# Attention output held in SBUF, and three 64-column products with v in place of a 64- and a 128-column one

## The chip, the cores and the metric

The kernel runs on one core of a Trainium2 chip. The metric is the device time of one execution in microseconds (us). Five engines work side by side, each on its own in-order stream of instructions: TensorE (PE, with its weight loads listed apart as PEld), VectorE (DVE), ScalarE (ACT), GpSimd (POOL) and SyncE (SP), which here issues every DMA.

## The reference

Attention with a memory term, followed by a two-layer network whose non-linearity is a squared relu. Four batches, eight heads, 576 positions, head width 64; 2304 tokens of width 512; hidden width 2048.

```python
scores = scale * np.matmul(q, k.transpose(0, 1, 3, 2))      # causal mask, then softmax -> a
local = np.matmul(a, v)
q_p = phi(q)                                                # elu + 1
mem_out = einsum(q_p, M_prev) / (einsum(q_p, z_prev) + 1e-6)
attn = g * mem_out + (1 - g) * local                        # g = sigmoid(beta)
x = attn.transpose(0, 2, 1, 3).reshape(B * S, H * D)
out = np.maximum(x @ w_in, 0.0) ** 2 @ w_out
```

Everything is float32. The kernel reaches that precision on 16-bit operands by splitting a number into a high and a low half and adding three products (high by high, low by high, high by low).

## The kernel before, in words

**Weights.** w_in and w_out come in 32 pieces of 512 KB. A piece is loaded by SP into a `raw` buffer (L269), its 64-bit words are put together to float32 by POOL or DVE (L192, L194), ACT (L195) and DVE (L198, into an `fc` buffer), and, once four pieces have a common scale (`weight_scale`), split into fp16 halves by ACT (L241) and DVE (L242). The `raw` and `fc` buffers come from two rings: the first eight pieces use a ring of 4 `raw` and 6 `fc` buffers; later pieces mostly use a second ring (`raw2`, `fc2`) in a pool that lies where the pool `tp` of the first tokens lay, so that its buffers wait for the end of `first_tokens`.

**First tokens.** The first 64 positions of every batch are computed apart (`first_tokens`, L319 to L391) and are block 0 of the network.

**Attention.** `attention(b, p, tiles, ...)` runs for a batch, a pair of heads and two or four query tiles of 128 rows; there are 24 such calls in `order`: batches 0 and 1 in two halves of two tiles, batches 2 and 3 whole. A call makes the memory term (`memx`, L520), then for each tile the scores (L543), mask and minimum (L564, DVE), exponential (L584, ACT), two fp16 halves `a` (L622 ACT, L624 DVE), a transposing DMA to `aT` (L628), the products with v (PE), and on DVE the division by the row sum and the addition to `memx` (L664). Six of the 64 tiles, those of the first three calls, take a float32 way (`full`); the other 58 are of the kind that the change touches. For those v has the halves `vh` and `vl` side by side in `vs`: per 64 or 128 keys the low half of `a` is multiplied with `vh` (64 columns, L651) and the high half with `vh` and `vl` together (128 columns, L649 and L654); `reduce_sum` (L656) adds the two 64-column parts into `s3`, from which L664 reads.

**Hand-over.** Each pair of finished tiles is written to a DRAM tensor `xd` (L675). `token_halves` reads a block of 256 tokens back (L699, L701), takes its scale (ACT L703, DVE L212 to L707), splits it (ACT L710, DVE L711) and transposes it by DMA into `xT` (L712). `moe(n)` calls it for block n + 1 at its step `PJ` = 6 of 8, and the block before the last two does it for both of those.

**Network.** `moe(n)`: first layer (L830 to L832, three products per k), relu, square, halves (L836 to L842), second layer (L802 to L804). Blocks 1 to 6 are done one by one, the last two together in `moe_pair` (L744 to L766).

**What sets the order.** The program text sets priorities: what is written earlier goes first when both can run. `ORD` interleaves the first attention calls with weight pieces (`wsteps`) and with `moe(0)`; then all other attention is written, then `moe(1)` on. A scheduler at build time turns that into one fixed order for each engine, in which network work fills what attention leaves free. At run time each engine keeps its order, and SP too: a DMA that has to wait holds up every DMA behind it.

Of the kernel before, what the change touches and what calls it, by code (L numbers as in the profile page):

```python
# [8 lines left out]
F32 = mybir.dt.float32  # L9
F32R = mybir.dt.float32r  # L10
# [40 lines left out]
NRAW = 4  # L51
NRAW2 = 2
NFC = 6
NFC2 = 6
NR0 = 8
# [4 lines left out]
EB = 3  # L60
RB = 2
KB = 2
XB = 4
PJ = 6
# [18 lines left out]
WE2 = 6  # L83
# [11 lines left out]
VB = 2  # L95
# [3 lines left out]
def fused_kernel(ctx: ExitStack, tc: tile.TileContext, t0_d, kk_d, qv_d, beta, w_in, w_out, out):  # L99
# [75 lines left out]
    xw = {}  # L175
# [10 lines left out]
    def to_float(n):  # L186
# [9 lines left out]
        pool, tag, bufs = (rwp, "fc", NFC) if first_ring(n, NFC, NFC2) else (more[0], "fc2", NFC2)  # L196
        fc[n] = pool.tile([P, 512], F32, tag=tag, name=tag, bufs=bufs)
# [40 lines left out]
    def halves(n, sc):  # L238
        f1 = fc.pop(n)
        hi, lo = wt[n][:, 0], wt[n][:, 1]  # L240
        nc.scalar.activation(hi, f1, AF.Copy, scale=sc)  # L241
        nc.vector.scalar_tensor_tensor(out=lo, in0=f1, scalar=sc, in1=hi, op0=ALU.mult, op1=ALU.subtract)  # L242
# [12 lines left out]
    wpl = ctx.enter_context(tc.tile_pool(name="wpl", bufs=1))  # L255
    rwp = ctx.enter_context(tc.tile_pool(name="rwp", bufs=1))
    more = []

    def first_ring(n, a, b):
        return n < NR0 or (n - NR0) % (a + b) >= b  # L260

    def load_weight(n):
        wt[n] = wpl.tile([P, 2, 512], F16, name=f"w{n}")
        if first_ring(n, NRAW, NRAW2):
            raw[n] = rwp.tile([P, 1024], U32, tag="raw", name="raw", bufs=NRAW)
        else:
            raw[n] = more[0].tile([P, 1024], U32, tag="raw2", name="raw2", bufs=NRAW2)
        w, r0, cs = wsrc[n]
        nc.sync.dma_start(raw[n], w[r0 : r0 + P, cs])  # L269
# [8 lines left out]
    def weights():  # L278
        with tc.tile_pool(name="tp", bufs=1, reuse_waits="tile") as tp:
            first_tokens(tp, ahead)  # L280
        more.append(ctx.enter_context(tc.tile_pool(name="rw2", bufs=1, reuse_waits="tile")))
        yield
        for n in range(NU):
            while len(loaded) < min(NU, n + NRAW + NRAW2):
                ahead()
# [10 lines left out]

    def first_tokens(tp, ahead):
        xT = mo.tile([P, 2, 2 * NK, P], F16, tag="xT", name="xT", bufs=2)
        xq.append((xT, tok0))
# [102 lines left out]
    dp = ctx.enter_context(tc.tile_pool(name="dp", bufs=1, space=bass.MemoryType.DRAM))  # L402
    xd = [dp.tile([S, DM], F32, name=f"xd{b}") for b in range(B)]
# [14 lines left out]
    def attention(b, p, tiles, ld, after, early, sfull, full):  # L418
# [13 lines left out]
        if not sfull:  # L432
            qh, ql = (at.tile([P, SQ], F32R, tag=t, name=t) for t in ("qh", "ql"))
            kh, kl = (at.tile([P, S], F32R, tag=t, name=t) for t in ("kh", "kl"))
# [14 lines left out]
        pe = at.tile([P, 2, S], F32, tag="e", name="pe", bufs=EB)[:, 0]  # L449
# [3 lines left out]
        if lead:  # L453
            later("s2", ex)
# [14 lines left out]
        if not full:  # L469
# [15 lines left out]
            vs = at.tile([P, 2, 5, 2 * D], F16, tag="vs", name="vs", bufs=1)  # L485
# [14 lines left out]
        memx = at.tile([P, 4, P], F32, tag="memx", name="memx", bufs=VB)  # L500
# [28 lines left out]
        done, started, a12 = set(), set(), None  # L529
        row = {}  # L530

        def scores(group):
# [20 lines left out]
            for (i, ka, kb), cs in zip(group, at_col):  # L553
                q0 = QT[i][0]
                if ka == 0:
                    row[i] = (
                        at.tile([P, 2, S], F32, tag="e", name="e", bufs=EB),
# [17 lines left out]
        for i in [t for t in TORD if t in tiles]:  # L575
# [31 lines left out]
            else:  # L607
# [4 lines left out]
                else:  # L612
                    a = at.tile([P, tg * P], F16, tag=f"a{tg}", name="a")
                    aT = at.tile([P, tg, P], F16, tag=f"aT{tg}", name="aT")
# [21 lines left out]
            acc = ps.tile([P, 2, 2, D], F32, tag="av", name="acc", bufs=2)  # L636
            if full:
                s3 = acc[:, :, 0]
                for h in range(2):
                    hd = slice(h * D, (h + 1) * D)  # L640
                    for c in range(nb):
                        kp = D if c == 0 else P
                        nc.tensor.matmul(
                            acc[:n, h, 0], aT[:kp, h * nb + c, :n], v[:kp, c, hd], start=c == 0, stop=c == i
                        )
            else:
                for h in range(2):
                    o2 = acc[:n, h].rearrange("p j d -> p (j d)")
                    nc.tensor.matmul(o2, aT[:, h * nb, :n], vs[:, h, 0], start=True, stop=i == 0)  # L649
                    for c in range(1, i + 1):  # L650
                        nc.tensor.matmul(  # L651
                            acc[:n, h, 0], aT[:, h * nb + i + c, :n], vs[:, h, c, :D], start=False, stop=False
                        )
                        nc.tensor.matmul(o2, aT[:, h * nb + c, :n], vs[:, h, c], start=False, stop=c == i)  # L654
                s3 = at.tile([P, 2, D], F32, tag="s3", name="s3", bufs=1)
                nc.vector.reduce_sum(out=s3[:n], in_=acc[:n].rearrange("p h j d -> p h d j"), axis=AX.X)  # L656
            if FX[late] == "p" and not full:
                xo = memx[:n, i - 1].rearrange("p (h d) -> p h d", h=2)
                smb = sm[:n, :, None].to_broadcast([n, 2, D])
                nc.gpsimd.tensor_tensor(out=s3[:n], in0=s3[:n], in1=smb, op=ALU.mult)  # L660
                nc.gpsimd.tensor_tensor(out=xo, in0=s3[:n], in1=xo, op=ALU.add)
            for h in range(2 if FX[late] != "p" or full else 0):
                xo = memx[:n, i - 1, h * D : (h + 1) * D]
                nc.vector.scalar_tensor_tensor(  # L664
                    out=xo, in0=s3[:n, h], scalar=sm[:n, h : h + 1], in1=xo,
                    op0=ALU.mult, op1=ALU.add,
                )
            fs = slice(p * P, (p + 1) * P)
            done.add(i)
            i0 = (i - 1) // 2 * 2 + 1  # L670
            if i0 in done and i0 + 1 in done and (b, p, i0) == (0, NP - 1, 1):
                last.append(memx)
            elif i0 in done and i0 + 1 in done:
                r0 = QT[i0][0]
# [14 lines left out]
    def token_halves(b, blk, xts, out_scale, tail=None):  # L689


        nk = NK if tail is None else NK - 1
# [3 lines left out]
        for t in range(2):  # L696
            r0 = QT[1 + 2 * blk + t][0]
            src = mo.tile([P, DM], F32, tag="x", name="xn", bufs=XB)
            nc.sync.dma_start(src[:, : nk * P], xd[b][r0 : r0 + P, : nk * P])  # L699
            if tail is not None:  # L700
                nc.sync.dma_start(src[:, nk * P :], tail[:, t])  # L701
# [16 lines left out]
    def prefetch(b, blk, tail=None):  # L718
        xT = mo.tile([P, 2, 2 * NK, P], F16, tag="xT", name="xT", bufs=2)
        osc = mo.tile([P, 2], F32, tag="osc", name="osc", bufs=2)  # L720
# [261 lines left out]
```

## Time and profile before

| what | value |
|---|---|
| runs | 598.8, 599.82, 603.67 us (median 599.82) |
| profiled execution | 604.48 us, of which the span of the trace is 602.7 us |
| PE busy | 543.7 us (90%) |
| DVE busy | 427.7 us (71%) |
| ACT busy | 376.8 us (63%) |
| POOL busy | 61.8 us (10%) |

A share of busy time is a mean over stages. The first stage (to about 150 us) prepares the weights, the middle one (to about 490 us) mixes attention and network, the last one is network alone. A busy PE includes the latency of its products, which overlap; the start-to-start distance of products tells what they cost.

### The profile page before, as it was taken

Reading aid. Unit: us, or ns where it says so; the run is one execution under the profiler, and the core shown is the slowest. Engines: PE = TensorE matmul, PEld = TensorE weight load, DVE = VectorE, ACT = ScalarE, POOL = GpSimd, SP = SyncE. Lnnn points to the kernel's source line nnn. Section 1 sums busy time; section 2 is a strip of 40 time slices with the busy share of each in tenths; the row PEclk is TensorE's granted clock in tenths of the full one; section 3 lists DMA queues with packets and bytes.
Section 4 is the critical chain, followed back from the end, with each engine's and each line's share of the span. In section 5 each row is a group of like instructions: output and inputs, shape, how many; then the busy total and the mean of one; then the engine's idle time right before and its main releaser. Section 6 shows DMA issues by size and latency. Waiting matters only on the chain.

```text
span 602.7 us, 11893 instructions
## 1 busy us (share of the span) xinstructions
PE 543.7 (90%) x4341; PEld 365.1 (61%) x4341; DVE 427.7 (71%) x1407; ACT 376.8 (63%) x831; POOL 61.8 (10%) x41
## 2 busy tenths in 40 slices
PE   6566988978989899998989999988999998999997
PEld 6455765645767666666666676656775775444443
DVE  6947888899986889799779696787977733222221
ACT  2535978559776868788688587588785634322223
POOL 2723872100010100000000000000000000000000
PEclk9975997889989999999999999999999999999999
DMA  8716962574966777796774764858826451000001
GB/s 315 258 63 202 369 203 75 141 146 93 187 136 142 131 161 148 151 173 129 203 149 114 123 149 103 163 129 184 158 54 112 109 131 36 35 1 1 0 2 71
DMA packets 141468, 79.08 MB, mean 131 GB/s; under 512 B 114016, under 2 KB 127584, under 8 KB 141408
## 3 DMA queue, kind: packets, MB, share of 16 engines
q1 hardware_dynamic: 141408, 78.31, 55.1%
q8 instruction: 34, 0.56, 0.4%
q14 instruction: 26, 0.21, 0.1%
HBM read 41.59 MB, written 8.78 MB: 84 GB/s over the span
## 4 chain that ended last, share of the span: by engine, by line
PE 31%; DVE 25%; DMA 21%; ACT 15%; issue 5%; SPq 1%; POOL 0%; DVEq 0%; ACTq 0%; POOLq 0%
PE oacc L744 7%; DMA aT<-a 4%; DMA vv<-in_qv_dram 4%; DVE e L564 4%; DMA xn<-xd 3%; ACT e L584 3%; DVE a L624 3%; DMA xd<-memx 2%; PE up L758 2%; PE up L757 2%; PE up L759 2%; ACT a L622 2%; DMA raw<-in_w_out_dram 2%; PE up L830 2%; PE oacc L802 2%
## 5 line engine op out<-in xcount | busy, mean ns | idle before, releaser
L830 PE MATMUL up<-xT,w 128*128 128x256 f16 x448 | 123.6, 276 | 0.9 <-DMA xT<-hl 0.8
L831 PE MATMUL up<-xT,w 128*128 128x256 f16 x448 | 123.6, 276 | 0.0
L832 PE MATMUL up<-xT,w 128*128 128x256 f16 x448 | 123.1, 276 | 0.0
L584 ACT ACTIVATE e<-e,mx 128x320 f32<-128x320 f32 (+3 forms) x128 | 77.5, 606 | 53.4 <-DVE memx L664 31.1
L802 PE MATMUL oacc<-w,gh 128*128 128x512 f16 x224 | 85.5, 384 | 9.5 <-ACT gh L839 5.5
L803 PE MATMUL oacc<-w,gh 128*128 128x512 f16 x224 | 86.1, 384 | 0.5 <-DVE w L242 0.5
L804 PE MATMUL oacc<-w,gl 128*128 128x512 f16 x224 | 83.0, 386 | 2.1 <-DVE gl L842 1.7
L624 DVE SCALAR_TENSOR_TENSOR a<-e,a 128x128 f16<-128x128 f32 x116 | 64.6, 566 | 25.9 <-ACT a L622 25.2
L622 ACT ACTIVATE a<-e 128x128 f16<-128x128 f32 x116 | 55.0, 522 | 11.2 <-DMA aT<-a 10.8
L830 PEld LDWEIGHTS <-w 128*128 128x128 f16 x448 | 44.3, 99 | 13.4 <-issue 2.3
L765 DVE CAST gh<-r 128x512 f16<-128x512 f32 x16 | 6.8, 428 | 62.0 <-ACT r L764 62.0
L831 PEld LDWEIGHTS <-w 128*128 128x128 f16 x448 | 44.4, 99 | 9.9 <-issue 0.3
L832 PEld LDWEIGHTS <-w 128*128 128x128 f16 x448 | 44.3, 99 | 8.7 <-issue 1.7
L192 POOL TENSOR_SCALAR raw<-raw 128x512 uint32<-128x512 uint16 x21 | 46.2, 2199 | 32.5 <-DMA raw<-in_w_in_dram 13.2
L564 DVE CUSTOM_DVE_ANT_0 e<-sp,mask 128x320 f32<-128x320 f32 (+3 forms) x128 | 47.4, 418 | 0.1
L842 DVE TENSOR_TENSOR gl<-r,gh 128x512 f16<-128x512 f32 x56 | 39.3, 702 | 10.9 <-ACT gh L839 10.4
L763 ACT ACTIVATE r<-up,gam 128x512 f32<-128x512 f32 x16 | 11.0, 687 | 57.2 <-PE up L759 57.2
L836 ACT ACTIVATE r<-up,gam 128x512 f32<-128x512 f32 x48 | 32.3, 672 | 17.5 <-PE up L832 17.5
L802 PEld LDWEIGHTS <-gh 128*128 128x128 f16 x224 | 22.1, 99 | 28.4 <-ACT gh L839 7.2
L804 PEld LDWEIGHTS <-gl 128*128 128x128 f16 x224 | 21.9, 99 | 27.5 <-DVE gl L842 5.2
L654 PE MATMUL acc<-vs,aT 128*128 128x128 f16 x302 | 37.3, 224 | 0.0
L651 PE MATMUL acc<-vs,aT 128*128 128x64 f16 x302 | 35.9, 196 | 0.0
(175 smaller groups left out, 1174.1 us busy)
## 6 DMA issues: line engine op xcount, KB each, us to landing
raw<-in_w_in_dram SPq DMA_DIRECT2D x16, 512.0 KB, 6.3
raw<-in_w_out_dram SPq DMA_DIRECT2D x16, 512.0 KB, 5.3
vv<-in_qv_dram SPq DMA_DIRECT2D x16, 320.0 KB, 3.0
kd<-in_kk_dram SPq DMA_DIRECT2D x16, 288.0 KB, 3.1
out_dram<-o SPq DMA_DIRECT2D x16, 256.0 KB, 2.8
xd<-memx SPq DMA_DIRECT2D x31, 128.0 KB, 2.3
xn<-xd SPq DMA_DIRECT2D x14, 256.0 KB, 3.0
qm<-in_qv_dram SPq DMA_DIRECT2D x8, 321.0 KB, 3.5
```

Source lines behind the costliest of these rows:

```text
L192: nc.gpsimd.tensor_scalar(out=u0, in0=top, scalar1=2.0**-13, scalar2=7.0, op0=ALU.mult, op1=ALU.min)
L564: nc.vector.tensor_tensor_reduce(out=e[:, h, ka:kb], in0=sps[:, h, cs], in1=mask[:, 448 - q0 + ka : 448 - q0 + kb], scale=-0.125, scalar=3 ...
L584: ex = nc.scalar.activation(e[:n, h, :ke], e[:n, h, :ke], AF.Exp, bias=bs, scale=-1.0, accum_out=sm[:n, h : h + 1])
L622: nc.scalar.mul(av[:, :, o0 : o0 + w], x, SC)
L624: nc.vector.scalar_tensor_tensor(out=av[:, :, o0 + w : o0 + 2 * w], in0=x, scalar=SC, in1=av[:, :, o0 : o0 + w], op0=ALU.mult, op1=ALU.sub ...
L744: mms.append(nc.tensor.matmul(acc[t], g[:, ts], w_out_op(f, part), start=s0, stop=s1))
L802: nc.tensor.matmul(acc[t], gh[:, u, ts], w_out_op(f, 0), start=f == f0, stop=False)
L803: nc.tensor.matmul(acc[t], gh[:, u, ts], w_out_op(f, 1), start=False, stop=False)
L804: nc.tensor.matmul(acc[t], gl[:, u, ts], w_out_op(f, 0), start=False, stop=f == f1)
L830: nc.tensor.matmul(up[:, u, :], w_in_op(f, k, 0), xT[:, :, k], start=k == 0, stop=False)
L831: nc.tensor.matmul(up[:, u, :], w_in_op(f, k, 0), xT[:, :, NK + k], start=False, stop=False)
L832: nc.tensor.matmul(up[:, u, :], w_in_op(f, k, 1), xT[:, :, k], start=False, stop=k == NK - 1)
```

## The change: what it does, and the diff

Three things are changed together.

1. `acc` is one group of 64 columns per head. All three products with v, for each stretch of keys, are 64 columns wide and add into the same columns; the high half of `a` is loaded as weights twice. `reduce_sum` is gone, and L664 reads `acc` from PSUM.
2. The attention output stays in SBUF: `memx` is a slice of a tile `feat[b]` that holds a batch, and `token_halves` reads it there. The DMAs of L675, L699 and L701 are gone. `prefetch` is called where the last head pair of a block is finished, in the text of attention, and no longer in `moe`.
3. To make room, the weight buffers are in pools that close: pieces 0 to 15 use a ring of 8 `raw` and 12 `fc` buffers that is open beside `tp`, pieces 16 to 31 a ring of 6 and 8 opened after it. What is free after that is the pool `late`, from which every second attention call after the fifth takes its work tiles (`e`, `a`, `aT`, `vs` and the halves of q and k). `ORD` takes 17 and 34 pieces where it took 13 and 33.

```diff
-NRAW = 4
-NRAW2 = 2
-NFC = 6
-NFC2 = 6
-NR0 = 8
+NRAW = 8
+NRAW2 = 6
+NFC = 12
+NFC2 = 8
+NR0 = 16
...
-WE2 = 6
+WE2 = 40
...
-    merge((attn(0, 1), 12), (wsteps(13), 12))
-    merge((attn(1, FIRST), 52), (wsteps(33), 20), (first(), 18))
+    merge((attn(0, 1), 12), (wsteps(17), 16))
+    merge((attn(1, FIRST), 52), (wsteps(34), 16), (first(), 18))
...
+    def weights():
+        with tc.tile_pool(name="rw", bufs=1) as rw:
+            more.append(rw)
+            with tc.tile_pool(name="tp", bufs=1, reuse_waits="tile") as tp:
+                first_tokens(tp, ahead)
+            yield
+            yield from pieces(0, NR0, NRAW)
+        wpl.append(ctx.enter_context(tc.tile_pool(name="wpl2", bufs=1, reuse_waits="tile")))
+        with tc.tile_pool(name="rw2", bufs=1, reuse_waits="tile") as rw:
+            more.append(rw)
+            yield from pieces(NR0, NU, NRAW2)
+        more.append(ctx.enter_context(tc.tile_pool(name="late", bufs=1, reuse_waits="tile")))
+        yield
...
-        memx = at.tile([P, 4, P], F32, tag="memx", name="memx", bufs=VB)
+        if b not in feat:
+            feat[b] = mo.tile([P, 4, DM], F32, tag="feat", name="feat", bufs=HB)
+        memx = feat[b][:, :, p * P : (p + 1) * P]
...
-                    o2 = acc[:n, h].rearrange("p j d -> p (j d)")
-                    nc.tensor.matmul(o2, aT[:, h * nb, :n], vs[:, h, 0], start=True, stop=i == 0)
...
-                s3 = at.tile([P, 2, D], F32, tag="s3", name="s3", bufs=1)
-                nc.vector.reduce_sum(out=s3[:n], in_=acc[:n].rearrange("p h j d -> p h d j"), axis=AX.X)
...
+            acc = ps.tile([P, 2, D], F32, tag="av", name="acc", bufs=2)
+            for h in range(2):
+                hd = slice(h * D, (h + 1) * D)
...
+                    mms = [(aT[:, h * nb], vh[:, 0]), (aT[:, h * nb], vl[:, 0])]
+                    for c in range(1, i + 1):
+                        hi, low = aT[:, h * nb + c], aT[:, h * nb + i + c]
+                        mms += [(low, vh[:, c]), (hi, vh[:, c]), (hi, vl[:, c])]
+                for x, (lhs, rhs) in enumerate(mms):
+                    nc.tensor.matmul(acc[:n, h], lhs[:, :n], rhs, start=x == 0, stop=x == len(mms) - 1)
...
-                xw[b, p, i0] = nc.sync.dma_start(
-                    xd[b][r0 : r0 + 2 * P, fs].rearrange("(i p) f -> p i f", p=P), memx[:, i0 - 1 : i0 + 1]
                 )
...
-            src = mo.tile([P, DM], F32, tag="x", name="xn", bufs=XB)
-            nc.sync.dma_start(src[:, : nk * P], xd[b][r0 : r0 + P, : nk * P])
+            src = feat[b][:, 2 * blk + t]
...
-            elif j == PJ and n + 1 < NBLK:
-                assert n > 0 or last
-                xq.append(prefetch(*blocks[n + 1], *last))
...
-            yield from attention(*order[i], ld, after, i < NEARLY, i < NES, i < NEF and max(order[i][2]) < 4)
+            yield from attention(*order[i], ld, after, i < NEARLY, i < NES, i < NEF and max(order[i][2]) < 4, more[-1] if i > FIRST and i % 2 else at)
+            b, p, tiles = order[i]
+            if p == NP - 1:
+                need(NU + 2)
+                for blk in range(2):
+                    if 2 * blk + 1 in tiles:
+                        prefetch(b, blk)
+                yield
```

The order of the DMAs on SP changes in the weight stage. Before (`raw` with a number is the second ring; `kd`, `qm`, `vv` are inputs of an attention call; in brackets the engines or DMA queues that the DMA waits for):

```order
L269 DMA raw<-in_w_in_dram 128x1024 [waits DMAHW7_49,DMAHW3_49,DVE_49]
L269 DMA raw<-in_w_in_dram 128x1024 [waits DMAHW0_49,DMAHW4_49,DVE_49,Activation_49]
L269 DMA raw<-in_w_out_dram 128x1024 [waits DMAHW1_49,DMAHW5_49,DVE_49,Activation_49]
L269 DMA raw<-in_w_out_dram 128x1024 [waits DMAHW6_49,DMAHW2_49,DVE_49]
L408 DMA kd<-in_kk_dram 128x320 [waits PE_49]
L269 DMA raw_507<-in_w_in_dram 128x1024
L269 DMA raw_568<-in_w_in_dram 128x1024
L408 DMA kd<-in_kk_dram 128x320 [waits PE_49]
L412 DMA qm<-in_qv_dram 128x386 [waits DVE_49,DMAHW3_49,PE_49,Activation_49]
L269 DMA raw_644<-in_w_out_dram 128x1024 [waits DMAHW4_49,DMAHW0_49,DVE_49]
```

With the change (line numbers of the changed kernel: L266 is the load of a piece, L415 to L422 the inputs of attention):

```order
L266 DMA raw<-in_w_in_dram 128x1024 [waits DMAHW0_49,DVE_49]
L415 DMA kd<-in_kk_dram 128x320 [waits DMAHW1_49]
L419 DMA qm<-in_qv_dram 128x386 [waits DMAHW2_49]
L422 DMA vv<-in_qv_dram 128x384 [waits DMAHW3_49]
L266 DMA raw<-in_w_in_dram 128x1024 [waits DMAHW4_49,DVE_49]
L266 DMA raw<-in_w_in_dram 128x1024 [waits DMAHW5_49,DVE_49]
L266 DMA raw<-in_w_in_dram 128x1024 [waits DMAHW6_49,DVE_49]
L266 DMA raw<-in_w_out_dram 128x1024 [waits DMAHW7_49,DVE_49]
L266 DMA raw<-in_w_out_dram 128x1024 [waits DMAHW0_49,DVE_49]
L266 DMA raw<-in_w_out_dram 128x1024 [waits DMAHW1_49,DVE_49]
L266 DMA raw<-in_w_out_dram 128x1024 [waits DMAHW2_49,DVE_49]
L415 DMA kd<-in_kk_dram 128x320 [waits PE_49]
```

Before, twelve pieces are issued ahead of the first `kd` that waits for PE; with the change sixteen are.

On DVE the same stage, around the first attention call. Before, six conversions of pieces (L198) stand behind that call's mask steps and its memory term (L514 to L520):

```order
L194 TENSOR_SCALAR raw_568<-raw_568 128x512
L514 SCALAR_TENSOR_TENSOR nm<-pm,gi 128x4
L518 RECIPROCAL nm<-nm 128x4
L520 TENSOR_TENSOR memx<-pm,nm 128x256
L198 SCALAR_TENSOR_TENSOR fc_641<-raw_507 128x512
L198 SCALAR_TENSOR_TENSOR fc_648<-raw_568 128x512
L198 SCALAR_TENSOR_TENSOR fc_655<-raw 128x512
L198 SCALAR_TENSOR_TENSOR fc_662<-raw 128x512
L198 SCALAR_TENSOR_TENSOR fc_704<-raw 128x512
L198 SCALAR_TENSOR_TENSOR fc_798<-raw 128x512
```

With the change (L196 is the conversion, L241 the low half of a weight, L573 the mask step, L392 and L395 steps of the first tokens) eight conversions, pieces 8 to 15, stand ahead of the call's first mask step:

```order
L392 TENSOR_TENSOR xs<-xp,sn 128x512
L241 SCALAR_TENSOR_TENSOR w_619<-fc,wout_s,w_619 128x512
L241 SCALAR_TENSOR_TENSOR w_622<-fc,wout_s,w_622 128x512
L196 SCALAR_TENSOR_TENSOR fc<-raw 128x512
L471 SCALAR_TENSOR_TENSOR pe<-qm,pe 128x256
L196 SCALAR_TENSOR_TENSOR fc<-raw 128x512 x7
L395 TENSOR_TENSOR xT<-xs,xT 128x512
L225 TENSOR_REDUCE win_e<-gr 128x1
L573 ISA e,mx<-sp,mask 128x320
```

## Rows read from the trace of the kernel before

**Rows 1.** The page, part 1: busy us (share of the span) and count.

```profile
PE 543.7 (90%) x4341; PEld 365.1 (61%) x4341; DVE 427.7 (71%) x1407; ACT 376.8 (63%) x831; POOL 61.8 (10%) x41
```

**Rows 2.** Busy time of each engine by stretch, with granted clock, DMA share, GB/s.

```profile
core 0: us, PE busy (x) PEld busy (x) DVE busy (x) ACT busy (x) POOL busy (x), PEclk, DMA share, GB/s
0.00:60.00 60.00, 37.67 (x479) 31.83 (x480) 41.82 (x110) 25.30 (x52) 23.92 (x20) 0.82 0.60 209
60.00:160.00 100.00, 88.28 (x669) 63.34 (x669) 90.58 (x285) 76.26 (x175) 32.84 (x18) 0.91 0.64 172
160.00:500.00 340.00, 319.15 (x2718) 223.00 (x2716) 271.98 (x972) 245.60 (x560) 5.01 (x4) 0.99 0.67 139
500.00:603.00 103.00, 98.65 (x480) 46.89 (x480) 23.28 (x42) 29.66 (x46) 0.00 (x0) 0.99 0.07 21
```

**Rows 3.** Timeline of DVE, 27 to 56 us: start, us, instruction [idle before <-releaser].

```profile
29.71 0.68 DVE L198 SCALAR_TENSOR_TENSOR fc<-raw 128x512 uint32<-128x512 uint32 x1
...
45.06 0.29 DVE L212 TENSOR_SCALAR qn<-nm 128x128 uint32<-128x128 uint32 x1 [5.68 <-PE nm L380]
...
53.89 2.69 DVE L198 SCALAR_TENSOR_TENSOR fc<-raw 128x512 uint32<-128x512 uint32 x4
```

**Rows 4.** Waits of the SP queue in the first 60 us: total, times, longest.

```profile
SPq L408 <- PE nm L380: 14.3, 1, 14.3
```

**Rows 5.** Waits of PE between 160 and 500 us.

```profile
PE oacc L802 <- ACT gh L839: 3.5, 5, 1.6
...
PE pm L509 <- DVE s L656: 1.5, 3, 0.6
PE vt L478 <- DVE s L656: 1.0, 2, 0.8
...
PE up L830 <- DMA xT<-hl: 0.8, 1, 0.8
```

**Rows 6.** Groups by line and shape: busy us, mean ns of one, idle before.

```profile
L656 DVE TENSOR_REDUCE s<-acc 128x128 f32<-128x256 f32 x58 | 24.3, 419 | 1.6
L664 DVE SCALAR_TENSOR_TENSOR memx<-s,sm,memx 128x64 f32<-128x64 f32 x116 | 28.3, 285 | 0.8
L664 DVE SCALAR_TENSOR_TENSOR memx<-acc,sm,memx 128x64 f32<-128x64 f32 x12 | 2.8, 275 | 0.0
L649 PE MATMUL acc<-vs,aT 128*128 128x128 f16 x116 | 24.8, 222 | 5.6 <-DMA aT<-a 3.2 <-DVE memx L520 1.6 <-DVE sm L633 0.5
L651 PE MATMUL acc<-vs,aT 128*128 128x64 f16 x302 | 35.9, 196 | 0.0
L654 PE MATMUL acc<-vs,aT 128*128 128x128 f16 x302 | 37.3, 224 | 0.0
```

**Rows 7.** Timeline of PE around 304 us: the products of two tiles with v.

```profile
304.03 0.22 PE L649 MATMUL acc<-vs,aT 128*128 128x128 f16 x1 [0.17 <-DVE memx L520]
304.09 0.19 PE L651 MATMUL acc<-vs,aT 128*128 128x64 f16 x1
304.12 0.22 PE L654 MATMUL acc<-vs,aT 128*128 128x128 f16 x1
304.17 0.19 PE L651 MATMUL acc<-vs,aT 128*128 128x64 f16 x1
...
304.71 0.22 PE L654 MATMUL acc<-vs,aT 128*128 128x128 f16 x1
304.76 0.27 PE L831 MATMUL up<-xT,w 128*128 128x256 f16 x1
```

**Rows 8.** Timeline of PE at 33.7 us: small products, each with its own weight load.

```profile
33.71 1.15 PE L367 MATMUL px<-ident,w 64*64 64x64 f32 x32
```

**Rows 9.** Waits of all engines: those at the hand-over.

```profile
ACT hl L703 <- DMA xn<-xd: 17.6, 8, 5.6
...
DVE ss L212 <- ACT hl L703: 15.0, 4, 6.1
```

**Rows 10.** Timeline of DVE around 394 us: the last attention step of batch 2.

```profile
394.93 0.48 DVE L664 SCALAR_TENSOR_TENSOR memx<-s,sm,memx 128x64 f32<-128x64 f32 x2
```

**Rows 11.** Timeline of PE: block 1 begins at 154 us, block 5 at 402 us.

```profile
154.07 0.27 PE L830 MATMUL up<-xT,w 128*128 128x256 f16 x1
...
402.16 0.27 PE L830 MATMUL up<-xT,w 128*128 128x256 f16 x1 [0.83 <-DMA xT<-hl]
```

**Rows 12.** The page, part 6: DMA issues, KB each, us to landing.

```profile
raw<-in_w_out_dram SPq DMA_DIRECT2D x16, 512.0 KB, 5.3
...
xd<-memx SPq DMA_DIRECT2D x31, 128.0 KB, 2.3
xn<-xd SPq DMA_DIRECT2D x14, 256.0 KB, 3.0
```

More of the change, by code (lines that the diff above doesn't have):

```diff
@@ L60 @@
 EB = 3
+EB2 = 3
 RB = 2
 KB = 2
-XB = 4
-PJ = 6
+XB = 3
 SEQ = 'a0 g a1 r r c0 l r r c1'
@@ L195, in to_float @@
         put(n, "s", nc.scalar.activation(f1, f1, AF.Prelu, scale=2.0**-111, alpha=-(2.0**32)))
-        pool, tag, bufs = (rwp, "fc", NFC) if first_ring(n, NFC, NFC2) else (more[0], "fc2", NFC2)
-        fc[n] = pool.tile([P, 512], F32, tag=tag, name=tag, bufs=bufs)
+        fc[n] = ring(n, "fc", [P, 512], F32, NFC, NFC2)
         nc.vector.scalar_tensor_tensor(
@@ L239, in halves @@
         f1 = fc.pop(n)
+        wt[n] = wpl[-1].tile([P, 2, 512], F16, name=f"w{n}")
         hi, lo = wt[n][:, 0], wt[n][:, 1]
@@ L276, in ahead, with pieces @@
             loaded.append(1)
[L278 to L284, printed above, removed]
+    def pieces(n0, n1, look):
+        for n in range(n0, n1):
+            while len(loaded) < min(n1, n + look):
                 ahead()
@@ L400, in first_tokens @@
                 outputs(g)
-    dp = ctx.enter_context(tc.tile_pool(name="dp", bufs=1, space=bass.MemoryType.DRAM))
-    xd = [dp.tile([S, DM], F32, name=f"xd{b}") for b in range(B)]
+    feat = {}
     def loads(b, p, tiles):
@@ L416, in loads, with attention @@
         return kd, qm, vv
-    def attention(b, p, tiles, ld, after, early, sfull, full):
+    def attention(b, p, tiles, ld, after, early, sfull, full, ap):
         q_eng, k_eng = (nc.gpsimd if c == 'p' else nc.vector for c in (EARLY if early else LATE))
@@ L447, in attention @@
             terms = [(q_raw, kd)]
-        pe = at.tile([P, 2, S], F32, tag="e", name="pe", bufs=EB)[:, 0]
+        pe = ap.tile([P, 2, S], F32, tag="e", name="pe", bufs=EB if ap is at else EB2)[:, 0]
         w = slice(qa, qb)
@@ L556, in scores @@
                     row[i] = (
-                        at.tile([P, 2, S], F32, tag="e", name="e", bufs=EB),
+                        ap.tile([P, 2, S], F32, tag="e", name="e", bufs=EB if ap is at else EB2),
                         at.tile([P, 2, 2], F32, tag="mx", name="mx", bufs=4),
@@ L663, in attention @@
+            for h in range(2):
                 xo = memx[:n, i - 1, h * D : (h + 1) * D]
                 nc.vector.scalar_tensor_tensor(
[L665 to L674, printed above, removed]
-                xw[b, p, i0] = nc.sync.dma_start(
-                    xd[b][r0 : r0 + 2 * P, fs].rearrange("(i p) f -> p i f", p=P), memx[:, i0 - 1 : i0 + 1]
+                    out=xo, in0=acc[:n, h], scalar=sm[:n, h : h + 1], in1=xo, op0=ALU.mult, op1=ALU.add
@@ L886, in fused_kernel @@
     blocks = [(None, 0)] + [(b, k) for b in range(B) for k in range(2)]
-    xq, last, behind = [], [], []
+    xq, behind = {}, []
     wg = weights()
```

102 lines of the change are left out of this document (34 added, 68 removed).

## The prediction, as it was put on record

> **What bounds the kernel now.** I read the page first. PE is busy 90% of the span, DVE 71%, ACT 63% [rows 1]: PE is the engine to look at, but it is the mean of very different stages. So the next view is busy time by stretch [rows 2]. In the last 103 us PE is busy 98.65 us and DVE 23: that stage is network alone, bound by PE, and nothing in the change touches it. From 160 to 500 us PE is busy 319.15 of 340 us, so 20.85 us are visibly idle, while DVE is busy 272 (80%) and ACT 246 (72%): PE is nearly full, and what it loses it loses waiting for in-order DVE and ACT. In the first 60 us PE idles 22.3 us, DVE is busy only 41.8 us, and the granted clock is 0.82: nobody is full, something else holds the weights. From 60 to 160 us DVE is busy 90.58 of 100 us: there DVE sets the pace.
>
> What holds the weights in the first 60 us is in two views. On DVE [rows 3] one conversion of a piece ends at 30.4 us and the next four come at 53.89; between them DVE is idle 5.68 us in one piece. On SP [rows 4] a `kd` load waits 14.3 us for PE at the end of the first tokens, and the loads of the next pieces stand behind it. Pieces 8 on need `fc` buffers in the memory of the first tokens, and pieces 12 on stand behind that `kd`.
>
> Network blocks follow each other without a gap in the order: block 1 begins at 154.07 us, block 5 at 402.16 us [rows 11]. So what is saved before 154 us reaches the end if the later blocks' tokens come earlier as well. Those of block 5 are the nearest case: batch 2's last attention step starts at 394.93 [rows 10], and the block's first product waits 0.83 us for its transposed tokens [rows 11].
>
> **The change, part by part.**
>
> *Weight rings (gain 7.5 us with the next part's share).* With 8 and 12 early buffers, pieces 8 to 15 need no memory of the first tokens, and sixteen loads are issued ahead of the `kd` that waits. Eight conversions move in front of the first attention call's mask steps. One of those four takes 2.69 / 4 = 0.67 us, so eight are 5.4 us of DVE, and they fit the idle piece of 5.68 us. They leave a stretch in which DVE is 91% busy, so I count them as path: 5.4 us. Bounds: a loss of 5.3 us, the landing of one piece [rows 12], if the last of them is late and DVE waits for it in front of attention; and a gain of 18.2 us, all the time DVE idles in the first 60 us (60 - 41.82 [rows 2]). The named gap is the nearest row, so I stay by it.
>
> *`reduce_sum` gone.* It is 58 x 419 ns = 24.3 us of DVE [rows 6]. Five of them fall before block 1 begins: 2.1 us, in the DVE-bound stretch, counted as path (so 5.4 + 2.1 = 7.5 us before 154 us). The other 53, 22.2 us, lie where PE is 94% busy, beside PE work. What is on the path there is what PE waits for: 1.5 + 1.0 us for `s` [rows 5]. L664 reads PSUM instead of SBUF: 275 ns against 285 in the two forms that are there already [rows 6], so nothing.
>
> *Hand-over in SBUF.* 31 writes and some 18 reads go, with 2.3 and 3.0 us to landing each [rows 12], and with them the time for which ACT stood still in front of L703, 17.6 us in eight waits, and DVE behind it, 15.0 us in four [rows 9]. Neither engine is the bound; PE sees it as late `gh` (3.5 us) and late `xT` (0.8 us) [rows 5]. I count both in full, since a stalled ACT holds every `gh` behind it. Together with the 2.5 us above: 6.8 us from 160 to 500 us. Bounds: nothing (work and transfers go and none comes, which excludes a loss), and the 20.85 us that PE idles in that stretch. I stay by the rows that name what goes away.
>
> *Products with v (cost 2.2 us).* Before: 302 times a 64- and a 128-column product, and 116 of 128 columns [rows 6]. A 64-column product is followed after 28 ns and a 128-column one after 56 [rows 7]: the 16 products from 304.03 to 304.76 us take 0.73 us, which is 6 x 28 + 10 x 56. So 302 x 84 + 116 x 56 ns = 31.9 us. After: 302 x 3 + 116 x 2 = 1138 products of 64 columns, 418 more products and weight loads than before. Their distance in an unbroken run is not in the trace: every 64-column product there is followed by a wider one [rows 7]. Nearest is a run of 32 products with a weight load each in 1.15 us [rows 8]; taking off the last one's 0.22 us leaves 31 steps of 30 ns. At 30 ns the new products are 34.1 us: +2.2. Bounds: 28 ns (nothing) and the 56 ns of a 128-column product (63.7 us: +31.8). I take 30, because that run pays for a load per product too. It all counts as path, since PE is nearly full there.
>
> The Trainium skill speaks against this step: "TensorE: Matmul & The Clock Gate", section "Back-to-back issue gap", gives about 81 ns per product for a steady stream of weight load and 128-column product. The trace has 56 ns for such pairs [rows 7], so the measurement decides. By the page's figure 418 more pairs would cost some 34 us (an estimate from that figure), and the kernel would be slower by about 20 us.
>
> *Two sets of attention work tiles, `prefetch` written earlier, 17 and 34 pieces.* These move work between calls; I find no row that prices them and count them at nothing. They are what would have to give the upper end of the gains.
>
> **Sum.** -7.5 - 6.8 + 2.2 = -12.1 us. The profiled execution took 604.48 us (its span and 1.8 us around it), which gives 592.4. It stands 4.7 us above the median of the runs, 599.82; against that median the sum is 587.7, and I forecast 588 us.
>
> **The rivals.**
>
> *A. Attention sets the pace, not PE.* Block 5 begins only when batch 2 is through attention, and batch 2's end stands 7 us in front of it [rows 10, 11]. If the chain of one attention call (mask, exponential, split, transposing DMA, products) does not shorten, PE's regained time turns into waiting for tokens. Against: each call loses 0.42 us per tile and gets a second set of work tiles. For: only 0.8 us of slack is missing now. Then half of the early gain stays, 3.8 us, less 2.2: 598 us, no change.
>
> *B. The narrow products come at the distance of wide ones (slower).* The place is every group of products with v from 154 to 490 us; the price is 1138 x (56 - 30) ns = 29.6 us on an engine that is full: 617 us. It decides from about 41 ns on, where 1138 x 11 ns eat the whole gain. For: each weight load has to fit in 28 ns behind another load. Against: the run at 30 ns [rows 8], and the load of a 128-column product that fits behind a 64-column one [rows 7]. The page's figure above points to this rival, and it has no other support here.
>
> *C. DVE's relief is on the path throughout.* If PE's idle time of 20.85 us went entirely and the first 60 us gave twice 5.4 us beside the 2.1, the sum would be -20.85 - 12.9 + 2.2 = -31.6: 568 us. For: DVE at 80% and ACT at 72% in fixed order lose more to each other than the named waits [rows 5], and two sets of tiles loosen that. Against: 24.3 us of DVE is 9% of its 272, not enough to end every wait.
>
> That the change does not do what it says can be left out: the order has no `reduce_sum` and no transfer with `xd`.
>
> **How the numbers follow.** The forecast's own range is 580 to 592 us (two thirds to one and a half times the gain of 14.3 us, less 2.2); chance 0.53. A has 0.20, B 0.13, C 0.13, and 0.01 is left for the early order below. The likeliest case gives the time, 588 us. For eight times in ten the range takes in A and two thirds of the way to C: 574 to 602 us; B lies outside. A measurement of this kernel tells about 1% from no change, that is 593.8 to 605.8 us as "within". Faster by over 1%: 0.49 of the forecast's 0.53, and C: 0.62. Slower: B, and 0.01 for an early order that loses its 5.3 us: 0.14. Within: A and what is left of the forecast, 0.24 with rounding.
>
> **What would show it.** In the changed profile: the gap between conversions at 30 to 54 us filled, the `kd` wait on SP without loads behind it, block 1 beginning near 146 us; DVE busy about 403 us; no wait of ACT in front of L703 on a DMA; the products with v about 30 ns apart; PE's idle time from 160 to 500 us at 14 us. A has block 5 waiting several us for its tokens; B shows in the distance of the products at once. I am wrong if block 1 does not begin earlier, or if it does and block 5 does not.

## The result and the profile after

The change takes 582.08 us (median of 4 runs, 578.94 to 584.73) against 599.31 us (4 runs, 596.34 to 603.67): ratio 0.9705, 95% interval 0.9627 to 0.9783. A second series gave 582.67 us and 0.970 (0.9655 to 0.9744). The forecast was 588 us, with a range of 574 to 602: the direction holds, and the gain is 17 us where the sum had 12; how the single terms fared is told below.

One warning for reading the two profiles side by side. That of before is the longest of its runs (span 602.7 us) and that of after the shortest (577.2), so the rows differ by 25.5 us where the medians differ by 17.2. Sizes below therefore come from medians; the rows say where. A second profile of the changed kernel (`after_again`, span 579.0 us) has block 1 at 130.31, batch 2's last step at 380.23 and block 5 at 383.09 us, as in the first (130.40, 380.53, 383.39).

The page of after, part 1, to be held against [rows 1]: 418 more products on PE, and DVE 22.1 us less busy.

```profile
PE 536.6 (93%) x4759; PEld 364.4 (63%) x4759; DVE 405.6 (70%) x1349; ACT 376.3 (65%) x831; POOL 58.7 (10%) x41
```

Busy time by stretch, with the columns of [rows 2]:

```profile
0.00:60.00 60.00, 43.45 (x540) 36.68 (x540) 50.47 (x144) 33.50 (x72) 24.44 (x20) 0.86 0.55 206
60.00:160.00 100.00, 91.55 (x773) 64.31 (x773) 88.63 (x278) 78.26 (x174) 32.20 (x19) 0.93 0.65 179
160.00:500.00 340.00, 328.36 (x3112) 230.37 (x3110) 250.81 (x901) 243.51 (x553) 2.08 (x3) 1.00 0.54 116
500.00:578.00 78.00, 73.28 (x340) 33.00 (x338) 15.66 (x28) 21.07 (x32) 0.00 (x0) 0.99 0.04 14
```

In the first 60 us DVE's idle time fell from 18.2 to 9.5 us; from 160 to 500 us PE's fell from 20.85 to 11.64 us. The second of these numbers varies: `after_again` has 14.93 us.

```profile
160.00:500.00 340.00, 325.07 (x3079) 227.85 (x3080) 250.67 (x899) 243.61 (x553) 1.88 (x2) 1.00 0.55 116
```

How the first came about shows on DVE, where [rows 3] had one conversion at 29.71 us and the next at 53.89 (six in a row, of which that row's window shows four), with 5.68 us of idle time in one piece between:

```profile
38.04 0.68 DVE L196 SCALAR_TENSOR_TENSOR fc<-raw 128x512 uint32<-128x512 uint32 x1
...
38.98 4.29 DVE L196 SCALAR_TENSOR_TENSOR fc<-raw 128x512 uint32<-128x512 uint32 x7
...
43.99 0.47 DVE L573 CUSTOM_DVE_ANT_0 e<-sp,mask 128x320 f32<-128x320 f32 x1
```

The eight conversions stand together ahead of the first mask step; the sixteenth piece is converted at 42.6 us where before it was 62.1. The `kd` loads on SP wait about as long as before (18.4 us; before 14.3 and 4.9), but no load of the first sixteen pieces stands behind them. SP's queue in the first 60 us, for [rows 4]:

```profile
SPq L415 <- PE sp L552: 18.4, 2, 15.9
SPq L266 <- DVE w L241: 12.2, 2, 11.3
```

The network's blocks and the last attention step of batch 2, for [rows 10, 11]. First PE: block 1's first product, block 4's last first-layer product, block 5's first.

```profile
130.40 0.27 PE L808 MATMUL up<-xT,w 128*128 128x256 f16 x1
...
370.66 0.27 PE L810 MATMUL up<-xT,w 128*128 128x256 f16 x1
...
383.39 0.27 PE L808 MATMUL up<-xT,w 128*128 128x256 f16 x1
```

Then DVE, the step from which block 5's tokens come:

```profile
380.53 0.47 DVE L660 SCALAR_TENSOR_TENSOR feat<-acc,sm,feat 128x64 f32<-128x64 f32 x2
```

Block 1 begins 23.7 us earlier (154.07 to 130.40), block 5 only 18.8 us (402.16 to 383.39). Block 4 issues its last first-layer product at 370.66, and block 5 starts 2.86 us after batch 2's last step; before, that distance was 7.2 us.

The products with v, on PE, for [rows 7]: 50 products of 64 columns in one run, each with its own weight load, and what follows them.

```profile
328.72 1.62 PE L657 MATMUL acc<-vs,aT 128*128 128x64 f16 x50
330.17 0.60 PE L782 MATMUL oacc<-w,gl 128*128 128x512 f16 x2
```

Fifty steps take 330.17 - 328.72 = 1.45 us, 29 ns each, which is also the median over the trace. 1138 x 29 ns are 33.0 us in place of 31.9. The division and addition read PSUM at 275 ns, as the twelve of [rows 6] did:

```profile
L660 DVE SCALAR_TENSOR_TENSOR feat<-acc,sm,feat 128x64 f32<-128x64 f32 x128 | 29.2, 275 | 3.5 <-PE acc L657 3.4
```

At the hand-over, ACT's waits from 160 to 500 us for [rows 9]. At that instruction (L703 before, L683 now) ACT no longer waits for DRAM, but it still waits 11.6 us there, where it was 17.6: for attention, or for the tile that a transposing DMA still reads.

```profile
ACT hl L683 <- DMA xT<-hl: 6.3, 2, 3.9
ACT hl L683 <- DVE feat L660: 5.3, 3, 2.8
```

### The profile page after: what moved, and what is told of

It reads as the page before. It is cut to its first block, busy times and chain, and to the rows that moved or that the text cites. A ratio compares the mean times of both kernels' runs of the same rounds, so it can differ in the third digit from the quotient of the medians.

```text
span 577.2 us, 12550 instructions
## 1 busy us (share of the span) xinstructions
PE 536.6 (93%) x4759; PEld 364.4 (63%) x4759; DVE 405.6 (70%) x1349; ACT 376.3 (65%) x831; POOL 58.7 (10%) x41
## 4 chain that ended last, share of the span: by engine, by line
PE 38%; DVE 17%; ACT 13%; DMA 12%; issue 3%; SPq 1%; ACTq 0%; DVEq 0%
PE oacc L722 7%; DMA vv<-in_qv_dram 5%; ACT e L593 4%; DMA aT<-a 4%; DVE a L633 4%; DVE e L573 4%; PE up L808 3%; PE up L810 3%; PE up L809 3%; PE oacc L781 3%; PE oacc L782 3%; PE oacc L780 3%; ACT a L631 3%; PE up L737 2%; PE up L736 2%
## 5 line engine op out<-in xcount | busy, mean ns | idle before, releaser
L782 PE MATMUL oacc<-w,gl 128*128 128x512 f16 x224 | 81.5, 382 | 1.9 <-DVE gl L820 1.6
L809 PEld LDWEIGHTS <-w 128*128 128x128 f16 x448 | 44.4, 99 | 11.6 <-issue 1.5
L657 PE MATMUL acc<-vs,aT 128*128 128x64 f16 x1138 | 44.4, 193 | 7.8 <-DMA aT<-a 5.2
L657 PEld LDWEIGHTS <-aT 128*128 128x128 f16 x1138 | 40.2, 98 | 16.0 <-DMA aT<-a 6.1
L573 DVE CUSTOM_DVE_ANT_0 e<-sp,mask 128x320 f32<-128x320 f32 (+3 forms) x128 | 47.0, 416 | 1.1 <-PE pxa L608 0.9
L191 POOL TENSOR_SCALAR raw<-raw 128x512 uint32<-128x512 uint16 x21 | 44.0, 2097 | 18.9 <-DMA raw<-in_w_in_dram 11.5
L814 ACT ACTIVATE r<-up,gam 128x512 f32<-128x512 f32 x48 | 32.4, 674 | 17.6 <-PE up L810 17.6
L782 PEld LDWEIGHTS <-gl 128*128 128x128 f16 x224 | 21.5, 98 | 24.3 <-DVE gl L820 3.6
```

Of the source, the lines that this page charges most:

```text
L191: nc.gpsimd.tensor_scalar(out=u0, in0=top, scalar1=2.0**-13, scalar2=7.0, op0=ALU.mult, op1=ALU.min)
L573: nc.vector.tensor_tensor_reduce(out=e[:, h, ka:kb], in0=sps[:, h, cs], in1=mask[:, 448 - q0 + ka : 448 - q0 + kb], scale=-0.125, scalar=3 ...
L657: nc.tensor.matmul(acc[:n, h], lhs[:, :n], rhs, start=x == 0, stop=x == len(mms) - 1)
L782: nc.tensor.matmul(acc[t], gl[:, u, ts], w_out_op(f, 0), start=False, stop=f == f1)
L809: nc.tensor.matmul(up[:, u, :], w_in_op(f, k, 0), xT[:, :, NK + k], start=False, stop=False)
```

## The experiments

All ratios are to the kernel before, run in the same series on the same chip, with 95% intervals. Series 1 held `small_rings`, `dram_handover`, `one_set` and `two_groups` (before: 598.64 us); series 2 `before_one_group`, `after_dve_pass`, `sbuf_and_writes` and `after_again` (602.08); series 3 `free_block5`, `split_batch2`, `before_split_batch2` and `inputs3` (598.9). Unless the name begins with before, the edit is made to the changed kernel.

### The parts taken back one at a time

**small_rings**: the first ring with as few buffers as before (it still serves sixteen pieces, where before it served eight).

```diff
-NRAW = 8
+NRAW = 4
-NFC = 12
+NFC = 6
```

> The changed kernel with the early rings cut from 8 raw and 12 fc buffers to 4 and 6, all else kept. If the gain was made by the weight rings ahead of block 1 (in the two profiles block 1 of the network begins 23.7 us earlier), block 1 goes back from 130 us to about 150 and the time to 590 to 598 us. If the gain comes from the relief of DVE or the hand-over, block 1 stays within 5 us of 130 and the time within 4 us of 582.

Measured: 594.67 us, 0.991 (0.9875 to 0.9944). That is 12.0 us above `after_again`, or by the two ratios 2.1% of 599 us = 12.6 us. The conversions on DVE spread out again, the first of these rows being piece 8 and the last piece 16:

```profile
28.32 0.68 DVE L196 SCALAR_TENSOR_TENSOR fc<-raw 128x512 uint32<-128x512 uint32 x1
...
57.08 0.69 DVE L196 SCALAR_TENSOR_TENSOR fc<-raw 128x512 uint32<-128x512 uint32 x1
```

and on PE block 1 begins 16 us later than in the changed kernel, block 5 only 8 us later:

```profile
146.36 0.27 PE L808 MATMUL up<-xT,w 128*128 128x256 f16 x1
...
391.46 0.27 PE L808 MATMUL up<-xT,w 128*128 128x256 f16 x1
```

Batch 2 is ready here at 378.1 us, 13.3 us ahead of block 5: attention is early and the network late.

```profile
377.92 0.47 DVE L660 SCALAR_TENSOR_TENSOR feat<-acc,sm,feat 128x64 f32<-128x64 f32 x2
```

Block 4's last first-layer product is issued at 389.27 us, 2.2 us ahead of block 5, so up to there PE's own work sets the pace.

**dram_handover**: the output of attention goes through DRAM again; `prefetch` stays where the change put it.

```diff
-            src = feat[b][:, 2 * blk + t]
+            src = mo.tile([P, DM], F32, tag="xn", name="xn", bufs=4)
+            nc.sync.dma_start(src, xd[b][r0 : r0 + P, :])
...
+                nc.sync.dma_start(xd[b][...], memx[:, i0 - 1 : i0 + 1])
```

> The changed kernel with the hand-over put back through DRAM (each pair of tiles written, each block read back; the prefetch stays where the change put it). If what it saves is what TensorE sees of late gh and late xT, 4.3 us come back: about 586 us, and ACT waits again for the read, some 15 us in all. If the hand-over is the main part of the gain, over 590 us. If nobody waits for it, 582 within 2 us.

Measured: 598.87 us, 1.000 (0.9972 to 1.0027): 16.2 us above `after_again` (3.0% by the ratios, 18 us). With this part alone taken back the whole gain is gone. Of ACT's waits from 160 to 500 us, the one that the change had taken away is back:

```profile
ACT hl L693 <- DMA xn<-xd: 12.3, 6, 5.2
```

Its landings are 2.2 us for a write and 3.1 us for a read (medians), and the longest wait is close to the sum. The Trainium skill, "DMA: Bandwidth & Descriptors", section "Anatomy of one DMA — SWDGE (gpsimd) path", gives a fixed cost of about 2.0 us beside the bytes, for transfers on another path; those here are issued by SP, and 2.2 us for 128 KB lies near it. PE's two starts here:

```profile
135.54 0.27 PE L818 MATMUL up<-xT,w 128*128 128x256 f16 x1
...
401.55 0.37 PE L818 MATMUL up<-xT,w 128*128 128x256 f16 x1 [0.79 <-DMA xT<-hl]
```

Batch 2's last step is at 393.02 us, 12.5 us later than in the changed kernel, and the way from it to block 5 takes 8.5 us in place of 2.9. Block 1, too, begins 5.1 us later.

```profile
393.02 0.47 DVE L660 SCALAR_TENSOR_TENSOR memx<-acc,sm,memx 128x64 f32<-128x64 f32 x2
```

Why batch 2 is late is less plain. Of the 12.3 us only 4.6 lie ahead of that step, and the changed kernel stands there about as long up to its own (2.5 us for attention, 2.3 for a transposing DMA). What grew most on that way is ACT's wait for `qm`, the q of the attention calls. First this run, 160 to 393 us, with a wait of SP's queue in which a read stands until the write before it has landed and later loads stand behind; then the changed kernel, 160 to 380.5 us:

```profile
ACT qh L444 <- DMA qm<-in_qv_dram: 22.8, 11, 4.6
ACT hl L693 <- DMA xn<-xd: 4.6, 4, 2.0
SPq L691 <- DMA xd<-memx: 6.9, 4, 2.9
...
ACT qh L442 <- DMA qm<-in_qv_dram: 13.7, 9, 2.6
```

That points at late inputs rather than at ACT's stand in front of the tokens; no run separates the two.

**sbuf_and_writes**: the 32 writes come back, but nobody reads them; the tokens stay in SBUF.

```diff
+                nc.sync.dma_start(xd[b][...], memx[:, i0 - 1 : i0 + 1])
```

> The changed kernel with the 31 or 32 writes of the attention output to DRAM put in again, which nobody reads; the hand-over stays in SBUF. If dram_handover lost its 16 us to the load on SP's queue and the DMA engines, at least half of them are lost here: 590 us or more. If it lost them to the round trip (a write, then a read in front of ACT's L703), 582 within 3 us.

Measured: 585.98 us, 0.9747 (0.9709 to 0.9785), 3.3 us above `after_again`. The two intervals nearly meet, so 3 us is a rough size. It is what the writes and their places in SP's queue cost; the other 13 of the 16 us come with the reads and with what waits for them. ACT's wait for `qm` does not grow with the writes alone: up to batch 2's last step (378.5 us) it is 8.2 us. Block 5 begins here at 381.39 us, 2 us earlier than in the changed kernel, although the run is the slower one.

```profile
381.39 0.27 PE L818 MATMUL up<-xT,w 128*128 128x256 f16 x1
```

**one_set**: every attention call uses the one set of work tiles.

```diff
-            yield from attention(*order[i], ..., more[-1] if i > FIRST and i % 2 else at)
+            yield from attention(*order[i], ..., at)
```

> The changed kernel with a single set of attention work tiles, so no call uses the pool called late. Counted at nothing in the prediction: 582 within 3 us. If the second set is what lets calls overlap, 587 or more, with block 5 and the last attention step later by as much and block 1 unmoved at 130 us.

Measured: 592.26 us, 0.988 (0.9849 to 0.9911): 9.6 us above `after_again`. Batch 2's last step on DVE comes 7.3 us later than in the changed kernel,

```profile
387.80 0.47 DVE L660 SCALAR_TENSOR_TENSOR feat<-acc,sm,feat 128x64 f32<-128x64 f32 x2
```

and block 5 on PE begins at 393.01, 9.6 us later:

```profile
393.01 0.27 PE L808 MATMUL up<-xT,w 128*128 128x256 f16 x1
```

Block 1 begins at 135.23 us, 4.8 us later, where the expectation had it unmoved. A part that the sum had at nothing is worth about 10 us.

**two_groups**: the old products (64 and 128 columns), `s3` and `reduce_sum`.

```diff
-            acc = ps.tile([P, 2, D], F32, tag="av", name="acc", bufs=2)
+            acc = ps.tile([P, 2, 2, D], F32, tag="av", name="acc", bufs=2)
...
+                s3 = ap.tile([P, 2, D], F32, tag="s3", name="s3", bufs=1)
+                nc.vector.reduce_sum(out=s3[:n], in_=acc[:n].rearrange("p h j d -> p h d j"), axis=AX.X)
```

> The changed kernel with the old products with v (64 and 128 columns, then reduce_sum and a sum tile in SBUF). By the prediction 2.1 us before block 1 and 2.5 us after come back and 2.2 us of products go: about 584.5 us. If VectorE's 24.3 us are on the path throughout, 595 or more. If the narrow products cost more than they save, under 580.

Measured: 586.24 us, 0.9788 (0.9754 to 0.9821): 3.6 us above `after_again`, 5 by the ratios. The products' own price argues for a gain of 1.1 us, so the cost lies elsewhere; the next two runs ask whether it is the DVE pass. Block 5 begins 9.4 us later than in the changed kernel, far more than the run loses:

```profile
392.79 0.28 PE L822 MATMUL up<-xT,w 128*128 128x256 f16 x1 [0.64 <-DMA xT<-hl]
```

### The DVE pass and the products by themselves

**after_dve_pass**: one more pass of DVE over `acc`, as long as `reduce_sum` was.

```diff
+                s3 = ap.tile([P, 2, D], F32, tag="s3", name="s3", bufs=1)
+                nc.vector.tensor_reduce(
+                    out=s3[:n], in_=acc[:n, :, :, None].to_broadcast([n, 2, D, 2]), axis=AX.X, op=ALU.max
+                )
```

> The changed kernel with 64-column products, but with a pass of DVE over each acc put in again (a maximum over a repeated axis, which copies acc to a tile in SBUF, 128x256 elements read like reduce_sum). If DVE's relief is what the product part gains, it loses as much as two_groups or 1 to 2 us more: 585 to 588 us where the changed kernel takes 582. If the gain of that part is in the products, 582 within 2 us.

Measured: 581.81 us, 0.9671 (0.9627 to 0.9714). The pass takes what [rows 6] gave for `reduce_sum`,

```profile
L662 DVE TENSOR_REDUCE s<-acc 128x128 f32<-128x256 f32 x58 | 24.3, 419 | 2.0
```

and the time does not move. 24.3 us of DVE are free in the changed kernel, so the loss of `two_groups` is not in the length of that pass. Nor is it in `s3` as a single buffer, which this run has as well. Whether it is in the products, in the wider `acc` or in the other order that the scheduler makes stays open.

**before_one_group**: only the products, in the kernel before.

```diff
-            acc = ps.tile([P, 2, 2, D], F32, tag="av", name="acc", bufs=2)
+            acc = ps.tile([P, 2, D], F32, tag="av", name="acc", bufs=2)
...
-                nc.vector.reduce_sum(out=s3[:n], in_=acc[:n].rearrange("p h j d -> p h d j"), axis=AX.X)
```

> The kernel before with only the products changed: one group of 64 columns, no reduce_sum, all else as before. By the prediction 2.1 + 2.5 us gained and 2.2 lost: 596 to 597 us where the kernel before takes 598.6. If VectorE's 24.3 us are on the path by themselves, 585 or less. If the products help only where attention sets the pace, no change within 2 us.

Measured: 608.16 us, 1.0108 (1.0069 to 1.0146): 1.1% slower. On PE block 1 begins 16.9 us earlier than in the kernel before, block 5 only 2.5 us:

```profile
137.20 0.27 PE L816 MATMUL up<-xT,w 128*128 128x256 f16 x1 [1.10 <-ACT r L822]
...
399.70 0.27 PE L816 MATMUL up<-xT,w 128*128 128x256 f16 x1 [1.09 <-DMA xT<-hl]
```

PE idles 27.6 us from 160 to 500 us, where it was 20.85,

```profile
160.00:500.00 340.00, 312.44 (x3016) 219.55 (x3016) 248.29 (x906) 240.76 (x551) 2.73 (x3) 0.99 0.65 135
```

and its waits there are now for attention:

```profile
PE acc L648 <- DMA aT<-a: 8.3, 6, 2.3
PE acc L648 <- DVE memx L520: 4.0, 5, 1.4
```

Batch 2 is ready at 391.7 us where the kernel before had 395.1, and block 5 moves with it, not with block 1. Why the run ends later than before although block 5 starts earlier is not settled: from that start to the start of PE's last product it is 200.5 us, in the kernel before 196.2.

One thing more is in this trace. The rings are those of before, and so is the gap: a conversion at 29.00 us, the next at 52.19. Block 1 begins 16.9 us earlier all the same, because the scheduler has made another order: 340 instructions of DVE (115.12 us) stand ahead of it, where before it was 379 (126.90 us), and only four of those were `reduce_sum`.

```profile
0.00:137.20 137.20, 106.06 (x1050) 81.94 (x1051) 115.12 (x340) 91.88 (x205) 55.85 (x36) 0.90 0.64 202
```

So every edit here changes the order as well, and no run holds the order fixed: a price from taking a part back contains both.

**after_again**: the changed kernel, for comparison in series 2.

> The changed kernel as it is, on the same chip as the others of this call, so that they can be compared with it: 582 us within 3, a ratio of 0.970 within 0.005 to the kernel before; in the trace block 1 begins at 130 us within 3 again.

Measured: 582.67 us, 0.970 (0.9655 to 0.9744).

### Who holds block 5

**free_block5**: block 5 takes tokens that are ready long before, those of batch 1's second block (so 256 rows of the output are not those of the reference; the work is the same). Its `prefetch` moves forward with them.

```diff
-            src = feat[b][:, 2 * blk + t]
+            src = feat[1 if (b, blk) == (2, 0) else b][:, 2 * blk + t]
```

> The changed kernel in which block 5 of the network reads batch 1's second token block instead of batch 2's first, so that it need not wait for batch 2's attention (its 256 output rows are those of other tokens; the work is the same). If attention of batch 2 gates block 5 in the changed kernel (there it starts 2.7 us behind the last attention step and 13 us behind block 4's last first-layer product), the time falls by 5 to 10 us to 572 to 577. If TensorE is the bound there, 582 within 2 us.

Measured: 577.79 us, 0.9645 (0.9601 to 0.969): 4.3 us under the median of after, 4.9 under `after_again`. On PE block 5 now follows block 4 at once:

```profile
370.73 0.27 PE L810 MATMUL up<-xT,w 128*128 128x256 f16 x1
...
373.43 0.27 PE L808 MATMUL up<-xT,w 128*128 128x256 f16 x1
```

while batch 2's last step is at 376.95. So with the change attention does hold block 5. Block 5 begins 10 us earlier than in the changed kernel and the end moves by about half of that; there PE did not stand idle meanwhile. Between block 4's first layer and block 5 it was busy 9.90 of 12.46 us, with block 4's second layer and with attention (the changed kernel, columns as in [rows 2]):

```profile
370.93:383.39 12.46, 9.90 (x102) 6.13 (x100) 9.26 (x36) 9.52 (x27) 0.00 (x0) 1.00 0.64 121
```

**split_batch2** and **before_split_batch2**: batch 2 in two halves, so that the first is ready early, in the changed kernel and in the one before.

```diff
-SEG = 2
+SEG = 3
```

> The changed kernel with batch 2's attention in two halves of two query tiles, like batches 0 and 1 (20 calls where it was 16 up to there, 28 in all), so that block 5 needs half of it only. If attention gates block 5, it starts 10 us earlier or more; four more calls cost DVE and ACT some 3 us each beside other work: 574 to 580 us. If TensorE is the bound, the added work shows: 584 or more.

> The same split in the kernel before. There block 4's last first-layer product (396.7 us) stands 5.5 us in front of block 5 and only 1.6 us behind batch 2's last attention step, so both would gate: at most 5 us to gain, and four more calls to pay: 596 to 602 us. If attention alone set its pace, 590 or less.

Measured: 594.34 us, 0.989 (0.9836 to 0.9945), and 607.49 us, 1.0122 (1.0068 to 1.0176). Each is slower than its own kernel: the first lands in its expectation's second case (584 us or more), the second above its whole range. In the first, block 5 starts at 373.9 us as in `free_block5`, yet from 160 to 500 us PE is busy 316.84 us where after has 328.36:

```profile
160.00:500.00 340.00, 316.84 (x3021) 224.99 (x3021) 256.33 (x932) 242.11 (x563) 2.29 (x3) 0.98 0.56 118
```

So it is not work added to PE, the reason given for that second case, that shows. In the second, block 5 begins 10.3 us earlier than in the kernel before, and the end comes 8.6 us later:

```profile
391.88 0.27 PE L830 MATMUL up<-xT,w 128*128 128x256 f16 x1
```

The further calls cost more than the early tokens bring; which part of them does was not tried.

**inputs3**: three buffers for the inputs of attention, paid for with a smaller first ring.

```diff
-QB = 2
-VVB = 2
+QB = 3
+VVB = 3
-NRAW = 8
+NRAW = 7
-NFC = 12
+NFC = 10
```

> The changed kernel with three buffers instead of two for q with M and for v (room from the early rings: 7 raw and 10 fc buffers). In the changed kernel ACT waits 16.7 us for q and DVE 14.2 us for v. If those waits lie in the attention chain that gates block 5, several come back: 574 to 579 us. If not, or if the smaller rings eat it, 581 to 586.

Measured: 584.69 us, 0.9734 (0.9683 to 0.9786): not apart from after, and in the second case of its expectation (581 to 586).

Of the versions that compute the reference none is clearly faster than the change.

## Why the prediction was right, step by step

**What bounds the kernel**: right. PE is the engine that ends last, and what it loses from 160 to 500 us fell (20.85 to 11.64 us, 14.93 in `after_again`; the prediction had 14).

**Weight rings, 5.4 us**: the mechanism is seen, the size was too small. The gap of [rows 3] filled, `kd` kept its wait without the loads behind it, but block 1 came at 130.4 us where the text had 146. Two things make the difference. DVE's idle time before block 1 fell from 27.2 to 15.5 us: 11.7 us, about twice the named gap, since beside the wait for `nm` (6.1 us, gone) smaller ones shrank: for `gh` from 2.6 to 0.2 us, for `vv` from 1.8 to nothing, for the loads of pieces from 2.8 to 0.9. `small_rings` has 25.8 us of idle time there, so this part goes with the ring. And DVE does 12.0 us less work ahead of block 1, mostly attention steps that now stand behind it; 1.6 us of it is `reduce_sum`, the rest the sum did not have at all. This part can't be put down to the ring, since `before_one_group` has as little work there with the ring of before. `small_rings` gives back 12 us, midway between the 5.4 us and the upper bound named in the prediction, 18.2.

**`reduce_sum`, 2.1 + 2.5 us**: wrong. The time of the pass is worth nothing in the changed kernel (`after_dve_pass`, 581.81 against 582.67 us). PE's waits for `s` are gone, but PE then waits elsewhere. The first term is also miscounted: four passes stand before block 1, not five, which makes 1.6 us.

**Hand-over, 4.3 us**: the right part, and a size off by a factor of four: `dram_handover` gives back 16 us. The sum took what PE visibly waited for (`gh`, `xT`). With the DRAM way batch 2 is 12.5 us later, before the longer way of the tokens (8.5 us for 2.9) is added, and the sum had neither. ACT's 17.6 us in front of L703 [rows 9] are near the 16 in size, but they are not shown to be the cause: ACT still stands 11.6 us at that instruction with the change, and in `dram_handover` what grew most ahead of batch 2's end was its wait for q.

**Products, +2.2 us at 30 ns**: right; measured 29 ns and +1.1 us. Rival B (56 ns each) is refuted. The Trainium skill, "TensorE: Matmul & The Clock Gate", section "Back-to-back issue gap", gives 81 ns per pair of load and 128-column product in a real stream; the rows here have 56 ns [rows 7]. The same page of the Trainium skill, section "Wait — 56ns, not 53.3ns?", has a floor of about 25 ns for small products and 55.6 ns at 128 columns; the 29 ns here lie above that floor, and the 56 ns agree. That the products cost nothing visible is shown inside the change only; alone in the kernel before, with the new order, they went with a loss of 1.1%.

**Counted at nothing**: wrong for the second set of work tiles (10 us by `one_set`). The earlier `prefetch` and the 17 and 34 pieces were not tried by themselves.

**Rival A** had its place right and not its weight. Attention does hold block 5 in the changed kernel, by 4 to 5 us (`free_block5`), and in `before_one_group` A fits what happens from block 1 to block 5. It did not take the gain: the change brings the end of batch 2 forward as well, from 394.93 to 380.53 us.

**The total** came out near partly by luck: two terms were too small, one is worth nothing, one at nothing is worth 10 us, and the terms do not add. Taking back one part at a time costs 12.0 + 16.2 + 9.6 + 3.6 = 41 us, but all of them together are worth 17. A reason for it, argued from the traces: the network on PE and batch 2's attention meet at block 5, and the later of them decides when it begins. With the small ring PE is late by 13.3 us, with the DRAM hand-over or one set attention is late. Delay either side and most of the gain goes, so the parts cannot be added.

This account ends at block 5. What follows is not explained: `two_groups` begins block 5 9.4 us later than the changed kernel and ends 3.6 us later, `sbuf_and_writes` begins it 2 us earlier and ends 3.3 us later, `before_split_batch2` begins it 10.3 us before its own kernel and ends 8.6 us after it. How much of that is the order that the scheduler makes behind block 5, and how much the part taken back, no run separates.

## What to carry to other kernels

When two chains meet at one point, ask of every part of a change which chain it shortens: a part that helps one chain alone can be worth nothing (or less) without the part that helps the other, and prices of parts taken from single removals can add up to more than the whole. What the bounding engine shows of a wait elsewhere can be far too low a price (4.3 us for 16 here): look for what is queued behind the same transfers, on the DMA queue too. A pass on an engine that is busy 70% of the time need not be worth its length: look for the wait that goes with it, and test by adding the same pass again. And where a scheduler makes the order, compare the orders of two versions before a difference is put down to the edit.

## What the runs showed of the hardware that was not expected

Products of 64 columns, each with a weight load of its own, follow each other after 29 ns, 50 in a row, so the second load of the high half of `a` shows no time of its own beside the product that uses it. A DRAM round trip of 2.2 us for the write and 3.1 for the read, made of 32 writes and 16 reads, costs 16 us in a kernel whose PE is busy 93% of the span without it; by which wait is not shown. And 24.3 us more of DVE work left the time unchanged.
